# The norm of the third attention pair on VectorE, a new order of all work, and shifted operands of the 256-column products

## The chip, the cores and the metric

The kernel runs on one core of one Trainium2 chip. The time is device microseconds of one execution, and a kernel is compared by the median of its runs.

## The reference

Three stages follow each other: masked attention, a mixer of keys and receptance, and a block that mixes along the sequence and then along the channels. All inputs are float32 in value.

```python
scores = scale * np.matmul(q, k.transpose(0, 1, 3, 2))          # 4 x 8 heads, 576 x 64
scores = np.where(masks[None, :, :, :], scores, -1000000000.0)   # window 32, or 128 in steps of 4
attn = np.exp(scores - np.max(scores, axis=-1, keepdims=True))
attn = attn / (np.sum(attn, axis=-1, keepdims=True) + 1e-09)     # the norm
x = heads_side_by_side(np.matmul(attn, v))                       # 4 x 576 x 512
...
k = np.maximum(xk @ w_k, 0.0)                                    # xk, xr: x mixed with the row before
v = k * k @ w_v
y = (1.0 / (1.0 + np.exp(-(xr @ w_r)))) * v
...
u = y + (y.transpose(0, 2, 1) @ U @ V).transpose(0, 2, 1)
return u + np.maximum(u @ w_ch1, 0.0) @ w_ch2                    # 512 -> 2048 -> 512
```

## The kernel before

The work is recorded first and put in order afterwards. Every step of the program is an operation with its engine, its cost, and the keys that it reads and writes. `plan()` then issues all of them by one list schedule: each engine takes, among the next operations that are ready by a model of their times, the one with the lowest rank, and the ranks come from a long packed table, RANKED, with 3463 numbers. So RANKED sets what stands behind what on each of TensorE (PE), VectorE (DVE), ScalarE (ACT), GpSimd (POOL) and the DMA queue of SyncE (SP). Where the plan expects TensorE to wait over 350 ns, it puts products of a tile of zeros ahead of the next operation (L1707), 512 or 224 columns wide, for 0.8 of the expected wait; they write to a bank that is overwritten afterwards.

**Attention** works on units (a pair of heads of one batch element, cut into windows). The first four units go one by one: scores L854, transposes of the probabilities L907, the product with v L919. The later ones go two at a time: L955, L993, L1011. Between scores and transposes VectorE takes the row's minimum (L779), ScalarE the exponential with its sum (L788), VectorE the reciprocal (L793, L794), and one engine multiplies each window by it: `norm`, L797 to L805. On ScalarE that is one ACTIVATE for each of the eight windows (L800), on VectorE one TENSOR_TENSOR for each unit (L805). NORM_ENG[u // 2] names the engine, and its third entry covers units 4 and 5 alone, which are the first ones that go together.

**The mixer** runs over eight chunks of 288 columns. Its weights come as 64-bit floating point and are turned to 32 bits (L539 on VectorE, L540, L544 on ScalarE; wx is a whole weight of 512 columns). Chunk 0 is multiplied in plain float32 with whole weights (L1107, L1122, two passes of the array for each). For the other chunks weights and operands are split in a high and a low part, and a product is three passes: high weight by high operand, low by high, high by low (L1094, L1095, L1096). The sigmoid is L1156, one ACTIVATE over 1152 columns, and ScalarE loads a table ahead of it and another ahead of the next exponentials.

**The sequence mixing** takes y back from DRAM (ytmp, then yb by L1211 on SyncE's queue), transposes it (L1220), multiplies by U (L1238) and V (L1255), adds (L1263), and writes u to DRAM (uf). It is read back in blocks ub of two 256-column parts (L1295).

**The channel MLP** works on blocks of 256 columns (Q) with fewer products than the plain sum (a Strassen scheme). Its first layer is L1371 to L1373, its second L1459 to L1461, again high by high, low by high, high by low, each 128 x 128 weights by 256 columns. There are 3072 of these products, all after 339 us, and little else runs on TensorE from there on. The weights of column groups j with j % 4 < 3 lie in the mixer's weight pieces (wh, wl); those of the last group lie in two large tiles, box A and box B (names boxA, boxB). The moving operands lie in boxes raw, w64 (names boxraw, boxw), x, sig and B. `part(tag, i, unit, n)` cuts a box in units of 256 columns (1024 bytes), so that two operands of a product stand apart by a distance that, modulo 256 bytes, depends only on where the tiles begin. These beginnings follow from the sizes of the tiles allocated ahead of them; small pads (PADS) and a few unused columns set them.

## Time and profile before

| | us |
|---|---|
| three runs | 718.67, 718.71, 720.33 |
| median | 718.71 |
| the profiled execution | 722.05 |
| its span, first to last instruction | 720.3 |
| granted TensorE clock over the span, share of full speed | 0.998 |

The share of an engine's busy time is an average over stages that have different limits. So the windows and the waits of TensorE by stage are read beside the page, and the timeline where two starts are compared. The start of a TensorE product is recorded, its end is modelled; the pace of products is therefore taken from start to start.

### The profile page before, as it was taken

The numbers are of one execution on the slowest core, as the hardware profiler recorded it, in microseconds if no ns is written. First come the engines' busy times: TensorE is split into PE (matmuls) and PEld (weight loads), VectorE is DVE, ScalarE is ACT, GpSimd is POOL, SyncE is SP. The second block draws the span as 40 slices with busy tenths as digits, with TensorE's granted clock in tenths as the row PEclk, the third lists the DMA queues.
The fourth block names the chain that finished last, engine by engine and source line by source line (L and its number), as shares of the span: only waits on it lengthen the run. The fifth ranks groups of instructions, "written<-read, shape, count | busy, mean of one in ns | idle before, by whom it ended". The sixth has DMA issues, their size and how long they took to land.

```text
span 720.3 us, 19185 instructions
## 1 busy us (share of the span) xinstructions
PE 709.9 (99%) x7534; PEld 687.5 (95%) x7534; DVE 596.8 (83%) x1526; ACT 422.2 (59%) x1047; POOL 127.7 (18%) x164
## 2 busy tenths in 40 slices
PE   8999999999999999999999999999999999999997
PEld 6778999999999999999899999999999999999997
DVE  5888998788867645899998998999999899797953
ACT  5887886867685836275644543455486545454331
POOL 0101364646463724130000000000000000000000
PEclk9999999999999999999999999999999999999999
DMA  8976258776748430756546445552464114003222
GB/s 318 348 280 232 91 186 260 246 266 231 235 141 275 158 122 1 235 188 209 182 125 203 136 144 198 162 165 79 138 213 133 60 45 132 30 31 118 89 68 66
DMA packets 69979, 117.71 MB, mean 163 GB/s; under 512 B 6144, under 2 KB 41216, under 8 KB 69888
## 3 DMA queue, kind: packets, MB, share of 16 engines
q1 hardware_dynamic: 69888, 116.49, 48.8%
q8 instruction: 59, 0.97, 0.6%
q14 instruction: 32, 0.26, 0.1%
HBM read 85.00 MB, written 31.46 MB: 162 GB/s over the span
## 4 chain that ended last, share of the span: by engine, by line
PE 89%; DVE 5%; DMA 3%; issue 1%; ACT 1%; SPq 0%; DVEq 0%
PE psM L1094 10%; PE psM L1095 10%; PE psM L1096 10%; PE psM L1371 7%; PE psM L1372 7%; PE psM L1373 7%; PE psM L1122 4%; PE psS L1459 4%; PE psS L1460 4%; PE psS L1461 4%; PE psM L1460 4%; PE psM L1461 4%; PE psM L1459 3%; PE psS L1011 2%; PE psS L955 2%; PE psM L1107 1%
## 5 line engine op out<-in xcount | busy, mean ns | idle before, releaser
L1094 PE MATMUL psM<-xk,wh 128*128 128x288 f32 x336 | 100.3, 298 | 0.0
L1095 PE MATMUL psM<-xk,wl 128*128 128x288 f32 x336 | 99.1, 295 | 0.0
L1096 PE MATMUL psM<-xk,wh 128*128 128x288 f32 x336 | 99.0, 295 | 0.0
L1094 PE MATMUL psM<-k2s,wh 128*128 128x288 f32 x224 | 67.0, 299 | 0.0
L1095 PE MATMUL psM<-k2s,wl 128*128 128x288 f32 x224 | 66.1, 295 | 0.0
L1096 PE MATMUL psM<-k2s,wh 128*128 128x288 f32 x224 | 66.0, 295 | 0.0
L1094 PEld LDWEIGHTS psM<-xk,wh 128*128 128x128 f32 x336 | 63.2, 188 | 0.8
L1095 PEld LDWEIGHTS psM<-xk,wl 128*128 128x128 f32 x336 | 63.2, 188 | 0.2
L1096 PEld LDWEIGHTS psM<-xk,wh 128*128 128x128 f32 x336 | 63.2, 188 | 0.0
L1371 PE MATMUL psM<-boxraw,wh 128*128 128x256 f32 x198 | 55.9, 282 | 0.8 <-ACT hc L1441 0.5
L1373 PE MATMUL psM<-boxraw,wh 128*128 128x256 f32 x198 | 55.2, 279 | 0.0
L1372 PE MATMUL psM<-boxraw,wl 128*128 128x256 f32 x198 | 55.2, 279 | 0.0
L496 POOL TENSOR_TENSOR k2s<-k,k2s 128x288 fp32r<-128x288 f32 x49 | 42.9, 879 | 63.7 <-ACT k2s L501 24.0
L1461 PE MATMUL psS<-boxx,wh 128*128 128x256 f32 x192 | 53.7, 280 | 0.0
L1371 PE MATMUL psM<-boxw,wh 128*128 128x256 f32 x186 | 52.3, 281 | 0.2
L1373 PE MATMUL psM<-boxw,wh 128*128 128x256 f32 x186 | 52.0, 279 | 0.3 <-DVE boxw L498 0.3
L1372 PE MATMUL psM<-boxw,wl 128*128 128x256 f32 x186 | 51.8, 279 | 0.0
L788 ACT ACTIVATE pr<-pr,mn 128x64 f32<-128x64 f32 x144 | 48.0, 336 | 4.7 <-DVE mn L779 4.3
L496 POOL TENSOR_TENSOR xk<-m,xk 128x288 fp32r<-128x288 f32 x48 | 43.0, 905 | 36.2 <-ACT xk L501 26.1
L1094 PEld LDWEIGHTS psM<-k2s,wh 128*128 128x128 f32 x224 | 42.1, 188 | 0.6
L1170 DVE SCALAR_TENSOR_TENSOR k<-psM,rt 128x288 f32<-128x288 f32 x56 | 25.1, 454 | 20.9 <-ACT rt L1165 17.9
L1095 PEld LDWEIGHTS psM<-k2s,wl 128*128 128x128 f32 x224 | 42.1, 188 | 0.2
(255 smaller groups left out, 2486.6 us busy)
## 6 DMA issues: line engine op xcount, KB each, us to landing
w<-w2raw SPq DMA_DIRECT2D x32, 512.0 KB, 5.3
w<-w1raw SPq DMA_DIRECT2D x20, 512.0 KB, 7.3
w2f<-w SPq DMA_DIRECT2D x32, 256.0 KB, 3.5
ub<-uf SPq DMA_DIRECT2D x32, 256.0 KB, 3.3
ws<-w2f SPq DMA_DIRECT2D x24, 256.0 KB, 4.1
raw<-qk SPq DMA_DIRECT2D x16, 320.0 KB, 6.8
ytmp<-y SPq DMA_DIRECT2D x32, 144.0 KB, 2.1
yb<-ytmp SPq DMA_DIRECT2D x4, 1152.0 KB, 6.5
```

Of the source, the lines that this page charges most:

```text
L496: op("POOL", t, lambda: nc.gpsimd.tensor_tensor(out=out_(), in0=a(), in1=b(), op=ALU.subtract), r, w, 40, lock=True)
L788: nc.scalar.activation(pr[:, d : d + KW], pr[:, d : d + KW], AF.Exp, bias=mn[:, i : i + 1], scale=-1.0, accum_out=sm[:, i : i + 1])
L1094: nc.tensor.matmul(a, lhsT=wh, rhs=xh, start=start, stop=False)
L1095: nc.tensor.matmul(a, lhsT=wl, rhs=xh, start=False, stop=False)
L1096: nc.tensor.matmul(a, lhsT=wh, rhs=xl, start=False, stop=stop)
L1122: pe(2, MM1, lambda o=o, acc=accs[o]: nc.tensor.matmul(acc()[:, :HS], lhsT=whole_w[w]()[:, o * P : (o + 1) * P], rhs=cols(src, n), start=f ...
L1371: nc.tensor.matmul(a, lhsT=wh(*wi), rhs=xh(*ci), start=start and n == 1, stop=False, skip_group_check=True)
L1372: nc.tensor.matmul(a, lhsT=wl(*wi), rhs=xh(*ci), start=False, stop=False, skip_group_check=True)
L1373: nc.tensor.matmul(a, lhsT=wh(*wi), rhs=xl(*ci), start=False, stop=last, skip_group_check=True)
L1459: nc.tensor.matmul(a, lhsT=wh(*wi), rhs=xh(), start=start, stop=False, skip_group_check=True)
L1460: nc.tensor.matmul(a, lhsT=wl(*wi), rhs=xh(), start=False, stop=False, skip_group_check=True)
L1461: nc.tensor.matmul(a, lhsT=wh(*wi), rhs=xl(), start=False, stop=stop, skip_group_check=True)
```

## The change

The change has three parts: the norm of units 4 and 5 goes from ScalarE to VectorE; RANKED is a new table, and with it the whole order; and the sizes of a few tiles and the beginnings of the parts in box A (by 16 columns, 64 bytes) and box B (by 16 or 64 columns, 64 or 256 bytes) change.

```diff
-XCOLS = 584
+XCOLS = 592
-NORM_ENG = ("DVE", "DVE", "ACT", "DVE", "POOL")
+NORM_ENG = ("DVE", "DVE", "DVE", "DVE", "POOL")
 RANKED = (
-    'c-l3a2Y6M*635R?4+KK*AiadHgd#;iIwD1+i1gk&f*?&nsUq?~MXGe9NKvW;5J4dn=?GE<q)7>o<ldX}e*ZV;-S69P_w3Hj&d%=6PT6}o%yH5=j<blg-'
...
+    'c-l>y2Xs}%*2m9HZb%_?0|*Mz1w=r4?<&$1r6Wb8D@~Bzdy^(52m+5Hy?0Tnij+r{4$=t%p(G)s-Shqa?(^3A?pm|v%*>uWd-lxi*=26}bdD45IL<=SA'
...
-    mu_t = cp.tile([P, 24], F32, name="mu_t")[:, :8]
+    mu_t = cp.tile([P, 8], F32, name="mu_t")[:, :8]
...
-    PADS = ['w', 'pt']
+    PADS, PADW = ['w', 'pt'], {'w': 16, 'pt': 48}
...
-                    pool.tile([P, 16], F32, tag=f"pad{self.tag}", name=f"pad{self.tag}", bufs=1)
+                    pool.tile([P, PADW[self.tag]], F32, tag=f"pad{self.tag}", name=f"pad{self.tag}", bufs=1)
...
-        def __init__(self, home, c0, n):
-            self.home, self.c0, self.n = home, c0, n
+        def __init__(self, home, c0, n, shift=0):
+            self.home, self.c0, self.n, self.shift = home, c0, n, shift
...
-            return self.home()[:, self.c0 + a : self.c0 + (self.n if b is None else b)]
+            c0 = self.c0 + self.shift
+            return self.home()[:, c0 + a : c0 + (self.n if b is None else b)]
...
-    BOXES = {"A": (1, 4608), "B": (1, 4608), "raw": (4, 1280), "w64": (4, 1024), "x": (2, 2304), "sig": (1, 1152)}
+    BOXES = {"A": (1, 4624), "B": (1, 4672), "raw": (4, 1280), "w64": (4, 1024), "x": (2, 2304), "sig": (1, 1152)}
+    def SHIFT(tag, unit):
+        return 16 if tag == "A" else (16 if unit < 10 else 64) if tag == "B" else 0
...
-        return Part(boxes[tag, i], unit * Q, n * Q)
+        return Part(boxes[tag, i], unit * Q, n * Q, SHIFT(tag, unit))
...
-        return Part(x.home, x.c0 + a, b - a)
+        return Part(x.home, x.c0 + a, b - a, x.shift)
```

The distance of moving operand to weights, modulo 256 bytes, worked out from the addresses in the two programs as they are built, for the 3072 products of 256 columns:

| distance | before, first layer | before, second layer | after |
|---|---|---|---|
| 0 | 0 | 352 | 0 |
| 64 | 0 | 704 | 0 |
| 128 | 384 | 32 | 0 |
| 192 | 1152 | 448 | 3072 |

The first-layer products at 128 are those with weights in box A. For the 288-column products the distances are 64 and 192 in equal shares, in both.

The program's lines move by -1 up to L600, and by +3 from L620 on. The first place is TensorE at the start of the program, from the second product of zeros on (raw holds q, k and v of a unit, pr the probabilities, wx whole weights). Before:

```order
L1707 MATMUL psM<-zero 128x512 x2
L854 MATMUL psM<-raw 32x64 x20
L1707 MATMUL psM<-zero 128x512 x11
L854 MATMUL psM<-raw 32x64 x20
L907 MATMUL psS<-cst_t,pr 128x128 x3
L1707 MATMUL psS<-zero 128x512 x3
L919 MATMUL psS<-pts,raw 64x32 x20
L907 MATMUL psS<-cst_t,pr 128x128 x3
L854 MATMUL psM<-raw 32x64 x20
L1707 MATMUL psS<-zero 128x512 x3
L919 MATMUL psS<-pts,raw 64x32 x20
L907 MATMUL psS<-cst_t,pr 128x128 x3
```

After:

```order
L1710 MATMUL psM<-zero 128x512 x2
L857 MATMUL psM<-raw 32x64 x20
L1710 MATMUL psS<-zero 128x512 x9
L910 MATMUL psS<-cst_t,pr 128x128 x3
L857 MATMUL psM<-raw 32x64 x20
L922 MATMUL psS<-pts,raw 64x32 x20
L910 MATMUL psS<-cst_t,pr 128x128 x3
L857 MATMUL psM<-raw 32x64 x20
L1710 MATMUL psS<-zero 128x512 x2
L922 MATMUL psS<-pts,raw 64x32 x20
L1710 MATMUL psS<-zero 128x512 x3
L910 MATMUL psS<-cst_t,pr 128x128 x3
```

The transposes of unit 0 (L907, now L910) stand ahead of the scores of unit 2 (L854, now L857), and nine zero products stand ahead of them in place of eleven. The zero products in these rows are 19 before and 16 after; a few rows later three narrow ones (224 columns) are new.

The second place is ScalarE between 33 and 42 us of the trace, around the norm (rt and k are the first layer's results, pts the transposed probabilities, sg the sigmoid's tile). Before:

```order
L501 ACTIVATE sg<-psM 128x288 x4
L788 ACTIVATE pr,sm<-pr,mn 128x64 x8
L540 ACTIVATE wx<-wx 128x512
L800 ACTIVATE pr<-pr,sm 128x64 x8
L540 ACTIVATE wx<-wx 128x512
L1165 ACTIVATE rt<-psM 128x288
L540 ACTIVATE wx<-wx 128x512
L1165 ACTIVATE rt<-psM 128x288
L501 ACTIVATE pts<-psS 128x512
L1167 ACTIVATE k_693<-rt 128x288 x2
L1165 ACTIVATE rt<-psM 128x288
L1167 ACTIVATE k_693<-rt 128x288
```

After:

```order
L791 ACTIVATE pr,sm<-pr,mn 128x64 x4
L539 ACTIVATE wx<-wx 128x512
L791 ACTIVATE pr,sm<-pr,mn 128x64 x4
L539 ACTIVATE wx<-wx 128x512
L1168 ACTIVATE rt<-psM 128x288
L1170 ACTIVATE k_666<-rt 128x288
L1168 ACTIVATE rt<-psM 128x288
L1170 ACTIVATE k_666<-rt 128x288
L539 ACTIVATE wx<-wx 128x512
L500 ACTIVATE pts<-psS 128x512
L1159 ACT_TABLE_LOAD
L1159 ACTIVATE sg<-sg 128x1152
```

The eight L800 rows are gone (two TENSOR_TENSOR on VectorE take their place), and the sigmoid with its table load stands where before there were results of the mixer; before, it stands 20 rows further on, one row ahead of the conversion for which the second group of zero products is put in. A second table load, ahead of exponentials, stands nearer too. In the whole program ScalarE has 14 table loads after and 12 before.

The third place is TensorE where the sequence mixing of the last batch element meets the first products of the channel MLP. Before:

```order
L1373 MATMUL psM<-boxw_5527,wh 128x256
L1255 MATMUL psS<-vs,g 128x288 x4
L1707 MATMUL psS<-zero 128x512 x2
L1220 MATMUL psS<-cst_t,yb 128x128 x4
L1707 MATMUL psS<-zero 128x512 x6
L1238 MATMUL psS<-yh,us 128x512
L1238 MATMUL psS<-yl,us 128x512
L1220 MATMUL psS<-cst_t,yb 128x128 x8
L1371 MATMUL psM<-boxw_5337,wh 128x256
```

After:

```order
L1376 MATMUL psM<-boxw_5415,wh 128x256
L1258 MATMUL psS<-vs,g 128x288 x8
L1223 MATMUL psS<-cst_t,yb 128x128 x4
L1710 MATMUL psS<-zero 128x512 x5
L1241 MATMUL psS<-yh,us 128x512
L1241 MATMUL psS<-yl,us 128x512
L1223 MATMUL psS<-cst_t,yb 128x128 x4
L1374 MATMUL psM<-boxw_5370,wh 128x256
```

The eight products by V stand in one row rather than four and four, no zero products stand between them and the transposes of yb, and five rather than six stand behind these; of the twelve transposes that follow, four stand here and eight a few products later, where it was eight and then four. Ahead of this stretch, directly behind the last product of the mixer, eight transposes of the batch element before are added. On SyncE's queue two reads of ub stand ahead of the read of yb, where one stood.

## Rows read from the trace of the kernel before

**Rows 1.** page, busy time, share of the span and instructions of each engine.

```profile
PE 709.9 (99%) x7534; PEld 687.5 (95%) x7534; DVE 596.8 (83%) x1526; ACT 422.2 (59%) x1047; POOL 127.7 (18%) x164
```

**Rows 2.** page, the chain that ended last, by engine.

```profile
PE 89%; DVE 5%; DMA 3%; issue 1%; ACT 1%; SPq 0%; DVEq 0%
```

**Rows 3.** waits of PE: line, what it waited for, us in total, times, longest.

```profile
PE psM L1371 <- DVE hb L1421: 1.3, 1, 1.3
...
PE psS L1707 <- DVE us L1263: 0.9, 1, 0.9
```

**Rows 4.** windows: stretch, us, busy PE, PEld, DVE, ACT, POOL (instructions), granted clock, DMA, GB/s.

```profile
31.00:55.80 24.80, 24.80 (x362) 19.66 (x361) 19.60 (x81) 22.62 (x76) 1.43 (x3) 1.00 0.82 295
...
59.20:334.00 274.80, 274.80 (x3495) 267.82 (x3494) 213.65 (x640) 185.23 (x536) 121.24 (x150) 1.00 0.57 193
...
338.90:354.10 15.20, 13.25 (x84) 11.54 (x82) 14.03 (x33) 6.50 (x12) 0.00 (x0) 0.89 0.73 231
...
480.00:600.00 120.00, 120.00 (x1026) 119.95 (x1025) 113.02 (x230) 71.83 (x141) 0.00 (x0) 1.00 0.38 118
```

**Rows 5.** timeline of PE: start, us, line, output, moving and stationary operand, shape.

```profile
362.94 0.28 PE L1371 MATMUL psM<-boxw,boxA 128*128 128x256 f32 x1
...
364.26 0.28 PE L1373 MATMUL psM<-boxw,boxA 128*128 128x256 f32 x1
...
408.41 0.28 PE L1371 MATMUL psM<-boxw,wh 128*128 128x256 f32 x1
...
409.70 0.28 PE L1373 MATMUL psM<-boxraw,wh 128*128 128x256 f32 x1
...
538.01 0.28 PE L1371 MATMUL psM<-boxw,wh 128*128 128x256 f32 x1
...
539.26 0.28 PE L1373 MATMUL psM<-boxw,wh 128*128 128x256 f32 x1
...
705.00 0.28 PE L1459 MATMUL psS<-boxB,wh 128*128 128x256 f32 x1
...
713.48 0.28 PE L1459 MATMUL psM<-boxB 128*128 128x256 f32 x1
...
716.25 0.28 PE L1461 MATMUL psM<-boxB,boxA 128*128 128x256 f32 x1
```

**Rows 6.** timeline of PE, the start of the program: the zero products of L1707.

```profile
4.75 1.22 PE L1707 MATMUL psM<-zero 128*128 128x512 f32 x2
...
7.72 4.55 PE L1707 MATMUL psM<-zero 128*128 128x512 f32 x11
```

**Rows 7.** timeline of PE, the second group of zero products.

```profile
55.88 3.35 PE L1707 MATMUL psM<-zero 128*128 128x224 f32 x25
```

**Rows 8.** timeline of ScalarE just before that group.

```profile
52.46 1.28 ACT L1156 ACT_TABLE_LOAD   x1
...
53.75 1.16 ACT L1156 ACTIVATE sg<-sg 128x1152 f32<-128x1152 f32 x1
...
54.82 0.61 ACT L540 ACTIVATE wx<-wx 128x512 f32<-128x512 f32 x1
```

**Rows 9.** timeline of PE, from the last first-layer product to the channel MLP.

```profile
338.94 0.40 PE L1238 MATMUL psS<-yh,us 128*128 128x512 f32 x1
...
346.25 0.69 PE L1255 MATMUL psS<-vs,g 128*128 128x288 f32 x4
...
347.82 0.73 PE L1707 MATMUL psS<-zero 128*128 128x512 f32 x2 [0.88 <-DVE us L1263]
...
349.37 1.08 PE L1220 MATMUL psS<-cst_t,yb 128*128 128x128 f32 x4 [0.81 <-DMA yb<-ytmp]
...
350.10 2.90 PE L1707 MATMUL psS<-zero 128*128 128x512 f32 x6
```

**Rows 10.** timeline of ScalarE, the norm of units 4 and 5.

```profile
34.69 2.00 ACT L800 ACTIVATE pr<-pr,sm 128x64 f32<-128x64 f32 x8
```

**Rows 11.** timeline of VectorE, L805: instructions, shortest/median/longest ns, first and last start.

```profile
L805 DVE TENSOR_TENSOR pr<-pr,sm x2: 396/408/419, 45.5 to 45.8; 128x256 f32<-128x256 f32 x2
```

More of the change, by code (lines that the diff above doesn't have):

```diff
@@ new lines @@
+    'lG&4l1}j*ndZ84gB<5<s_RY-ah&b}*Zn5hb!WeH-2oXLry?*nf&G|N7`THeuG<rs9pH0)j`QM~>lUEAHPUf%0P_;~<4LaDkMxxC)GUtk3GKJzT=y%=*X'
+    'Xwvm{ue|>2K;f&|VX~QS@1r*>T<kZ>@OOJ;!*vp=%|8U-NwdTH{IK*&Jsy<5s5ckx<8(3GPpV9j6lgs)DmC6Rk(NI&-K9d~IMp<oj2~e#zV_0+$5b9@0'
+    'Q?Hz9Ya{|{*s{Zbh74zRB%cY&@-j6I6)3gDf|cWq$KB)V=S{OU!0N$?c~$3@MD@m>d}CTZ_0*DXcc-Sm$0QG)AUq2Fe{HP`8kv5UTS!BL<2H=yqq%;&W'
+    '*$GHw4&H&qm@>lfV2hIZ|(79Sa@s;Vg6Zj6Ly=(@@IUVb|3z%mO>iyyiV{E6rI^QM8-vI7U#;H#^*k^oy4H~C_cRXW70CNSJT2MEgy0@SU7C5uP(-Iy{'
+    'Bri-JLq8vI@sy`gzC&4ae@?!E{3T-~(7y<H8u8tl`aK|D3-M*3Z!P6%wD+Yy%jkSh-iz@^(msy?8&hr)u(?zP_8u@7$p1@f1-}XdGZOxsqx>n~=`}aU_'
@@ new lines @@
+    '}_}ULD04t+Uo&(6uc+ND+8AwhV5qFukkH@<aX>l^ro&Cc~(+-XzuBa*$5hQLdW;i{o>j$7i(UC_4yr~<+P8Pw9ZBd{O>}ax}>9wAI7*ffb9zGGUn3<Tr'
+    ';Sv53avRcPXdS*`aS!@?QeB-$v6Xg?SgI9M2r{(`OH``GLtzT?G721pipZxkh;p?dvFSA|-(L4s=~74}&Rt=>LP(k#vx{GQbz6-x1ORQW;V@Xv;`jUHa'
+    'Dtm&^A?#wtSkOtgaUFy9%$@tpDvzUx498TdP$wzc$I51v)zA47j-&TJ8wdW!Sd64^0?Js*l(2!&58$!9X*-i*_L?-s!S1Wm8Bmw@XH&fJXCntp@X3s0G'
+    'AbIM1OEiI;B8}cb^nu+vj2+T=nnnqq*`v}-;l*jW;=G+7KWb$gz`~;epP}aPneRkeAQ=Y|lGI$Ts_Y>A?C2)P<TZ0gjP0xV2#+-ECwI8wokJxeFqP_*+'
+    '%f0>l1F&zCIzmf5>PJ&IiE=yOeuS7I&?|&9$mdhn0Uj-8KmN`*I>)ckXD)3W$wBE<q^>yM9|OCabeXz1()-kxB>$aM8k)M%X9IPc!1IaZ5Mx|{&X)9jz'
@@ new lines @@
+    '&v7^Q-tJKu<eZ%AdjIw1^5e+b<h?I{^hg}23H-vGgG$(9NL=|sGmyzBYZcP+-Kc1_fw>IfeQxLAjasxyko$9l)OLdnpI<yPp40`)&_XVu<#J0`8IU!VX'
+    'v=-4`0H7e3Tc__730ksCxu$W2npR$>WyvDZqHy!F5dQMrz4-gCILQl4ozF+M4tQen-G$(j3ZrNsk%(Gs=HZUtDsP@_y18#ux*wWf{8&ZQ;NM$nTLCr>z'
+    '2gb^+Ipl$rYS%;_BPof-EGZ95tB19&qWI>%F2%x`B}b3O}vdio6j*CU^u>C)s8)P?FS>5c*ZCFM9z9+f5aqW|-N-L<nRPo}(_a!1k?zwz=0brtFVr?&@'
+    'YQNN5jj*ioWF}h2Jkq*)R8}KJ-Pa`h{oh!*Z(KZ+0JP`XXeP)sV>$AHf9drB=m?hxd&H9BRyMtMmi_m$6_T0ez>h&1_{uhz~z;A%wv5d2qJ_mulKwCp{'
+    'ofpZz%;b+H$En*1Y);WYzeAGie&h4c;QmHuhFtndd&ySPZTer(`cZ#dvX}38*6a#vF;ViEy|e|Hw~+aiV;{EDJpkON;A~F0A@zkaA@{)j9ecDn?UM67n'
@@ new lines @@
+    'cEBcj!v_4m4&(%;H!r`dH_ugC1+FYo=>m63?0P+CNsCvCzH+&FssS`q3sQLA^BMxJd!KD=u;Bd6~VSYF927E@{E9;(b~Xu2hT#<A2LRnS0=O0=ze4!-X'
+    'hIs9!<cLNWPkK1aO1-&dK-Z<beLWhTnld2AazPn*)5qs9VZd1GJx|+wol}*ksdF#_kE+WSw*PGY39SqrMLHUx8PAKLz{-=y^%s?C@k4@aY))Aow2ey_~'
+    'jP?4fn!C8%F4{y|SI^4*kk@!d7m?kt_F?2LU*GC+G;Iwy4-8RI+Ps*vk`eS>t1KKsZIQ<qotkvCw><KWo<o#S-(fTK3~IM(jtP}5x=(65N}FX;CJH&3#'
+    'iw)5g&km*5tp!EqbX_D3890u&uG@H*^<`@QSQ(#w-x=LT7yo-DieJAq$3&fA%`xC~l&Uj<MKU{p{z6+t8iGC^Is{{US(0fg?oiR>A&qLbR(JnbUfx7XM'
+    'C+xFN;o$@AA7Iy#X9p&Uaryw48T?J*+cPe(D$KPTx^y$}{{ikClz*cC{Y<7Kr_wJoeWrk;hwgImh5BZ|^#P^<c`fvmhR`}39IKf_EcFSTjgHJs^Jzo>('
@@ L200 @@
+    ';8S}9sMWbTm8pC@A#R^H{qracA<VzoV~>vLjU)fuXIcCO17omv+7;9VmyZ+c5#aR-{wHT-m%^YGF|4p-+VlMbq}SQO(avIs%PWr-Tkm+`=5+-qVnXQYp'
+    '#BKgMLhJWEEafESY}#@6$&<i#I;-?$Pjo`4&Ee_q#mVdd0CfTzWUM+_kp~(rJtM?fukY?Pb5kBlN!j>0JK@6A#w?'
 )
```

153 lines of the change are left out of this document (65 added, 88 removed).

## The prediction

> **What bounds the kernel now.** I read the page first. TensorE is busy for 709.9 of 720.3 us [rows 1], and the chain that ended last is TensorE for 89%, VectorE for 5%, DMA for 3% [rows 2]. So a gain must either shorten TensorE's own work or take away one of the few places where it stands. The windows tell these stages apart [rows 4]. In 59 to 334 us TensorE fills the stretch whole (274.80 of 274.80), and again in 480 to 600 us (120.00 of 120.00): there nothing but the pace of its products counts. In 338.9 to 354.1 us it is busy for 13.25 of 15.20 us at a granted clock of 0.89, so the time goes into waits, fillers and a fallen clock. The waits view names few others: the largest is 1.3 us for a hidden block hb on VectorE, then 0.9 us for us [rows 3]. In 31 to 55.8 us TensorE is never idle (24.80 of 24.80), while ScalarE is busy for 22.62 of them; that is where the norm stands which the change moves.
>
> **The pace of the 256-column products.** In 480 to 600 us, where TensorE never waits, 1026 products take 120.00 us, 117.0 ns each [rows 4]. Between single starts the pace isn't one number [rows 5]. Twelve first-layer products with weights in box A, at distance 128, run from 362.94 to 364.26: 1.32 us over 11 steps, 120.0 ns. Twelve at distance 192 run from 408.41 to 409.70, 117.3 ns, but twelve others at 192 from 538.01 to 539.26, 113.6 ns. Seventy-two at 64, second layer, run from 705.00 to 713.48, 117.8 ns; the 23 behind them, at 0, take until 716.25, 120.4 ns. I did the same for all 3071 starts of the trace (these rows are the firsts and lasts of five of the runs), and left out steps over 130 ns. First layer: 115.9 ns at 192 (1136 steps), 118.3 at 128 (380). Second layer: 116.8 at 192 (446), 117.8 at 64 (702), 118.7 at 0 (349). All together: 117.1 ns. Which box holds an operand doesn't separate them further; the distance does.
>
> The change puts all 3072 at 192. Like for like, layer by layer, that is 384 x 2.4 ns for those at 128, 352 x 1.9 for those at 0, 704 x 1.0 for those at 64: 0.9 + 0.7 + 0.7 = 2.3 us less. I take **-2.3 us**. The bounds: nothing (0), if the tiles happen to differ by something other than distance, and, on the far side, what the two paces inside 192 allow. Its steps lie either near 113.5 or near 117.7 ns, some 40% in the first, whole runs of twelve in one of them, with nothing in the addresses to decide which; at the borders of runs the pace changes over. All in the fast pace would be 3072 x (117.1 - 113.4) = 11.4 us less, all in the slow one 3072 x 0.6 = 1.8 us more. As 40% is also what the share of changes each way inside 192 would settle at by itself (a fast step is followed by a slow one in 17% of cases, a slow by a fast one in 11%, which gives 0.11 / 0.28), I see no push to either end.
>
> The rows say that distance counts, at equal columns. The Trainium skill speaks against this part of the change: its page "SBUF — State Buffer", section "SBUF: two separate sides", says that on the engines' side only the port pair that VectorE and GpSimd share makes anyone wait, and TensorE never does; "TensorE: Matmul & The Clock Gate", section "Back-to-back issue gap", gives the gap from the number of columns alone. By that this term would be 0 and the sum 2.3 us higher, as in the second rival; the five runs of these rows, all of 256 columns at full clock, do not agree with one gap.
>
> **The start.** Up to 31 us TensorE waits for loads and for the softmax of single units, and the planner's zero products stand in these waits. Of these 19 wide ones precede the mixer's first product, 16 in the new order, and three narrow ones are added. Eleven wide ones take 4.55 us [rows 6], 0.41 each; a narrow one 3.35 / 25 = 0.13 [rows 7]: -3 x 0.41 + 3 x 0.13 = -0.84 us. Fillers stand for waits, so part returns as a wait for what they stood for: raw data that have not landed, or the minimum and exponentials of a unit. The bounds are 0 and -1.2 (the wide ones alone, none of it coming back). I take **-0.7 us**, as the transposes of unit 0 come at once behind the nine, where two zero products and a set of scores lay between.
>
> **The norm and the chunk-0 stage.** The eight ACTIVATEs cost ScalarE 2.00 us [rows 10]. Two TENSOR_TENSORs of the same form on VectorE are 396 and 419 ns at 45.5 us [rows 11]: 0.82 us, in a stretch where VectorE has 24.80 - 19.60 us free [rows 4]. By itself this is worth nothing at 35 us, since TensorE is never idle from 31 to 55.8 us: the work of chunk 0 covers it. It counts where that cover ends, at 55.88, where 25 zero products take 3.35 us [rows 7] until a whole weight is converted at 54.82, behind a table load of 1.28 and a sigmoid of 1.16 us [rows 8]. In the new order the sigmoid is 20 rows further ahead, and 21 zero products stand at the stop, 4 x 0.13 = 0.5 us less. Against it, another table load and exponentials now stand ahead of the weight that is waited for. With the 2.00 us that ScalarE no longer spends, the stop can shrink further. Bounds: all of the 3.35 us gone, or, on the other side, 1.28 + 1.16 + 1.28 = 3.7 us more from what has been put ahead. I take **-1.0 us**, nearer to the fillers' own count than to the end. Two more table loads in the program, 2 x 1.28 us, cost nothing where ScalarE has slack: it is busy for 185 of 275 us in 59 to 334 us [rows 4].
>
> **The passage to the channel MLP.** From 338.94, TensorE has three products by U, 48 of the first layer, then four products by V from 346.25, and stands for the sums us (0.88 us and two zero products, 0.73); yb lands for the transposes at 349.37, 0.81 us after TensorE is ready, and six zero products take 2.90 us, 0.48 each at a fallen clock [rows 9]. Waits and fillers here are 0.88 + 0.73 + 0.81 + 2.90 = 5.3 us. In the new order the same work and eight transposes more come in a row: 48 x 0.116 + 0.7 (the products by U) + 2 x 0.69 + 8 x 0.09 (half of what one of the four from 349.37 to 350.10 takes at the fallen clock) = 8.4 us, to 347.3. If yb lands as it does now, 10.4 us behind 338.94, TensorE is idle for 2.0 us and then has five zero products, 2.4 us: 4.4 us, a gain of 0.9. The idle time is in one piece, unfilled, so the clock may fall earlier than now; I take **-0.6 us**. Bounds: -2 (yb released sooner) and +2 (yb behind two reads of ub on SyncE's queue, rather than one, and landing later). Later, the wait for hb and those for DVE's other blocks, some 3 us together up to 480 us, may move either way; the order alone doesn't tell, and I put them at 0 with 1.5 us to each side. VectorE is nearly full there (14.03 of 15.20, and 113.02 of 120.00 us [rows 4]), so a faster TensorE meets it sooner; in 480 to 600 us it has 7 us left, three times what the pace would take.
>
> The tail behind the last product is the same work, 0.
>
> **Sum.** -2.3 - 0.7 - 1.0 - 0.6 = -4.6 us. The profiled execution took 722.05 us and its span is 720.3; it lies 3.3 us above the median of the three runs, 718.71. Against its own time the sum is 717.4; against the median, to which the new median is compared, **714.1 us**.
>
> **Rivals.** First, the stream holds its fast pace. Products at other distances often throw it from one pace into the other now: all 31 + 13 fast steps that follow a change of distance from 192 to 0 or 128 are preceded by slow ones. Without such neighbours it might stay at 113.4: -11.4 - 2.3 = 705.0 us if throughout, about 709 if in two thirds of the steps. Against it: inside 192 alone it falls back as often as it rises.
>
> Second, the distance isn't what counts, and the first term is 0, or the stream holds the slow pace: 718.7 - 2.3 = 716.4 us, up to 718.2 with the slow pace. For it: two paces appear at one and the same distance, so that something else has a part. Against it: five means, from 350 to 1136 steps each, follow the distance in either layer.
>
> Third, the moves on ScalarE make it slower. Sigmoid, two table loads and four exponentials (some 5 us in all) stand ahead of the sixteenth weight, and the norm gives back only 2.00. If all of it comes behind the last zero product, TensorE stands for 5.0 us, unfilled, and its clock falls as it does in 338.9 to 354.1 us, where it costs some 1.7: with the other terms (-3.6) that is 718.7 - 3.6 + 5.0 + 1.7 = 721.8 us. It decides from a delay of about 4 us on. Against it: ScalarE has 2.2 us free in 31 to 55.8 us, and the sigmoid comes out of this very place.
>
> The change not doing what it says is no case here: the addresses and the order are those of the built program.
>
> **How the numbers follow.** Forecast 0.62, fast pace 0.13, pace term missing 0.18, slower through ScalarE 0.07. About 0.3%, 2.2 us, is what a measurement can tell from no change: below 716.5 is faster, above 720.9 slower. The forecast lies below 716.5 but for a few in a hundred, the second rival for a third: 0.59 + 0.13 + 0.06 = 0.78 faster, 0.15 within, 0.07 slower. The range leaves out the slower case, the upper half of the second rival and the fast pace beyond two thirds: 708.5 to 717.5 us.
>
> **What would show it.** Pace: 1026 products in 120.00 us become about 1034 per 120.00 in a stretch without waits, and start-to-start steps at one mean in both layers; if the mean stays at 117.0 the first term was wrong. Start: the mixer's first product comes 0.7 us earlier. Chunk 0: the second group of zero products ends with the product behind it starting at once. Passage: the time from the mixer's last product to the end of the zero products behind yb, now 350.10 + 2.90 - 338.94 = 14.1 us, is less by 0.6. It would be wrong above all if VectorE, nearly full up to 600 us, made new waits in the channel MLP.

## The result and the profile after

The changed kernel takes 714.28 us in the median of six runs (713.26 to 716.32), the one before 719.78 in the median of six (718.67 to 721.46). The ratio is 0.9918, with a 95% interval of 0.9899 to 0.9936: 5.9 us less, between 4.6 and 7.3. On another chip (e12_after, below) it was 0.9920 (0.9903 to 0.9937). Forecast was 714.1 us, 4.6 us less, range 708.5 to 717.5. The profiled executions lie further apart than the medians (spans 711.8 and 720.3 us); below, two things are shown in which single executions of one kernel differ, by some 2 us each.

The page of the changed kernel, its waits of TensorE (line, what it waited for, us in total, times, longest), and three windows of it (stretch, us, busy PE with instructions, granted clock, DMA share, GB/s); they answer to [rows 1], [rows 3] and [rows 4]:

```profile
PE 703.4 (99%) x7527; PEld 681.2 (96%) x7527; DVE 598.0 (84%) x1528; ACT 421.4 (59%) x1041; POOL 125.9 (18%) x164
```

```profile
PE psS L1258 <- DVE us L1266: 1.1, 1, 1.1
...
PE psS L1223 <- DMA yb<-ytmp: 0.6, 1, 0.6
PE psM L1374 <- DVE hb L1424: 0.5, 1, 0.5
```

```profile
410.00:520.00 110.00, 110.00 (x937) 1.00 0.50 160
668.00:707.00 39.00, 39.00 (x347) 1.00 0.22 67
...
480.00:600.00 120.00, 120.00 (x1025) 1.00 0.33 102
```

TensorE is still the bound. The first two windows hold nothing but 256-column products, all of them at distance 192, on a TensorE that never waits at full clock. In the first a product takes 110.00 / 937 = 117.4 ns, in the second 39.00 / 347 = 112.4 (from the starts in the timeline 117.8 and 113.3; a window counts products that it cuts). So one kernel, in one execution, at one distance, runs at two paces, and each for tens of microseconds: some 970 steps in a row in the first, 352 in the second. Before the change both appear too, but at 192 in runs of a dozen or two [rows 5].

The third window is the one that the prediction named as its sign for the pace: 1034 products were forecast there, 1026 stood there before [rows 4], and 1025 stand there now. By that sign alone the pace would not have changed. But two thirds of this window lie in two long runs at the slow pace (up to 521.7 us, and from 541.6 to 578.2); over all the steps counted below, the mean falls from 117.1 to 115.7 ns. In the second trace (e12_after) the same window has 1032.

Three places that the prediction had named, in the timeline of the changed kernel (start, us, engine, line, output, operands, count). The zero products at the start, the mixer's first product, and the three new narrow zero products, which stand behind it, against [rows 6]; then the mixer's first product before:

```profile
7.54 4.10 PE L1710 MATMUL psS<-zero 128*128 128x512 f32 x9
...
17.96 2.11 PE L1110 MATMUL psM<-xk,wx 128*128 128x288 f32 x8
...
21.59 0.57 PE L1710 MATMUL psM<-zero 128*128 128x224 f32 x3
```

```profile
19.02 2.11 PE L1107 MATMUL psM<-xk,wx 128*128 128x288 f32 x8
```

The second group of zero products and the product behind it, against [rows 7]; then the last step of the whole weight that this product reads, which is VectorE's, after and before, and the product before:

```profile
51.00 2.71 PE L1710 MATMUL psM<-zero 128*128 128x224 f32 x21
53.55 3.75 PE L1125 MATMUL psM<-k,wx 128*128 128x288 f32 x14
```

```profile
52.63 0.69 DVE L549 SCALAR_TENSOR_TENSOR wx<-w,wx 128x512 int32<-128x512 int32 x1
```

```profile
57.56 0.69 DVE L550 SCALAR_TENSOR_TENSOR wx<-w,wx 128x512 int32<-128x512 int32 x1
```

```profile
59.08 11.33 PE L1122 MATMUL psM<-k,wx 128*128 128x288 f32 x46
```

ScalarE ahead of it, against [rows 8]:

```profile
37.45 1.28 ACT L1159 ACT_TABLE_LOAD   x1
38.74 1.17 ACT L1159 ACTIVATE sg<-sg 128x1152 f32<-128x1152 f32 x1
...
48.67 1.28 ACT L791 ACT_TABLE_LOAD   x1
```

The passage to the channel MLP, against [rows 9]:

```profile
348.15 0.63 PE L1223 MATMUL psS<-cst_t,yb 128*128 128x128 f32 x4 [0.62 <-DMA yb<-ytmp]
348.54 1.41 PE L1710 MATMUL psS<-zero 128*128 128x512 f32 x5
```

The norm of units 4 and 5 is now two instructions of VectorE, ahead of where ScalarE did it [rows 10]:

```profile
33.50 0.42 DVE L808 TENSOR_TENSOR pr<-pr,sm 128x256 f32<-128x256 f32 x1
...
35.26 0.42 DVE L808 TENSOR_TENSOR pr<-pr,sm 128x256 f32<-128x256 f32 x1
```

### The profile page after: what moved, and what is told of

The parts are those of the page before. It is cut to its first block, busy times and chain, and to the rows that moved or that the text cites. A ratio compares the mean times of both kernels' runs of the same rounds, so it can differ in the third digit from the quotient of the medians.

```text
span 711.8 us, 19151 instructions
## 1 busy us (share of the span) xinstructions
PE 703.4 (99%) x7527; PEld 681.2 (96%) x7527; DVE 598.0 (84%) x1528; ACT 421.4 (59%) x1041; POOL 125.9 (18%) x164
## 5 line engine op out<-in xcount | busy, mean ns | idle before, releaser
L1376 PE MATMUL psM<-boxw,wh 128*128 128x256 f32 x186 | 51.9, 279 | 0.0
L1375 PE MATMUL psM<-boxw,wl 128*128 128x256 f32 x186 | 51.9, 279 | 0.0
L1097 PEld LDWEIGHTS psM<-k2s,wh 128*128 128x128 f32 x224 | 42.1, 188 | 0.4
L1099 PEld LDWEIGHTS psM<-k2s,wh 128*128 128x128 f32 x224 | 42.1, 188 | 0.0
```

The costliest lines, as they stand in the source:

```text
L1097: nc.tensor.matmul(a, lhsT=wh, rhs=xh, start=start, stop=False)
L1099: nc.tensor.matmul(a, lhsT=wh, rhs=xl, start=False, stop=stop)
L1375: nc.tensor.matmul(a, lhsT=wl(*wi), rhs=xh(*ci), start=False, stop=False, skip_group_check=True)
L1376: nc.tensor.matmul(a, lhsT=wh(*wi), rhs=xl(*ci), start=False, stop=last, skip_group_check=True)
```

## The experiments

### The parts apart: distance alone, order alone, distance 0

e1_addr is the kernel before with the beginnings of tiles changed and nothing else; every engine's order stays word for word. e2_order is the changed kernel with the tiles at their old places. e5_all0 is the changed kernel with all 256-column products at distance 0:

```diff
-    PADS, PADW = ['w', 'pt'], {'w': 16, 'pt': 48}
+    PADS, PADW = [], {}
-    BOXES = {"A": (1, 4624), "B": (1, 4672), ...
+    BOXES = {"A": (1, 4608), "B": (1, 4608), ...
-        return 16 if tag == "A" else (16 if unit < 10 else 64) if tag == "B" else 0
+        return 0
```

Expected of e1_addr: 

> The kernel before with the changed beginnings of tiles alone: every instruction stands where it stood on every engine, and all 3072 products of 256 columns are at distance 192. If the distance sets their pace, the mean step falls from 117.1 to the 115.7 ns that the changed kernel shows, 3072 x 1.4 = 4.4 us, and the median by 4 to 5 us; by my prediction's like-for-like term, 2.3 us. If the order decides whether the stream holds its fast pace, the second layer's mean stays near 116.8 ns and the gain near 2.3 us. If the distance is only a bystander, nothing changes.

Expected of e2_order: 

> The changed kernel with the tiles at their old places: new order and norm on VectorE, distances as before. If the distance is worth 4.4 us and the parts add, it is 1 to 2 us faster than before and some 4 us slower than the changed kernel; the start (1.0 us) and the passage to the channel MLP (1.4 us) come earlier as in the changed kernel's trace, and the mean step of the 256-column products is 117.1 ns. If the order makes the pace, the mean step is 115.7 ns and it is as fast as the changed kernel.

Expected of e5_all0: 

> The changed kernel, same instructions in the same order, with all 256-column products at distance 0 rather than 192 (the 288-column ones move too, from 64 and 192 to 0 and 128). If distance sets the pace, the mean step is 118.7 to 120 ns, so 3072 x 3 to 4.3 ns = 9 to 13 us more than the changed kernel, some 4 to 7 us over before. If uniformity is what helps (no neighbours at other distances), it is about as fast as the changed kernel. If neither, it equals the kernel with the old places, some 4 us over the changed one.

| kernel | median us | of before, with interval |
|---|---|---|
| e1_addr, old order, all at 192 | 720.3 (717.08 to 726.87, 12 runs) | 0.9992 (0.9968 to 1.0015) |
| e2_order, new order, old distances | 717.66 (717.25 to 719.75) | 0.9956 (0.9940 to 0.9973) |
| changed kernel | 714.28 | 0.9918 (0.9899 to 0.9936) |
| e5_all0, new order, all at 0 | 726.18 | 1.0070 (1.0047 to 1.0093) |

Distance 0 against 192, at the same order, is worth 1.0070 - 0.9918 = 1.5% of the time, some 11 us, as was expected of distance. About 1.6 us of it stands in the mixer (270.0 us against 268.4), where the 288-column products move too. The mean step of its 256-column products in the trace is 119.9 ns, and of 3042 steps only nine, never two in a row, are below 115.5. That no reading by uniformity alone can explain. The windows of its trace and of the one before (same columns), in stretches that TensorE fills whole, e5_all0 first:

```profile
480.00:600.00 120.00, 120.00 (x1000) 1.00 0.35 105
600.00:700.00 100.00, 100.00 (x835) 1.00 0.23 72
```

```profile
600.00:700.00 100.00, 100.00 (x855) 1.00 0.21 67
```

120.00 / 1000 is 120.0 ns, and 100.00 / 835 is 119.8, against 100.00 / 855 = 117.0 before.

The order alone gives 0.44%, 3.2 us. The distance on top of it gives 0.9956 - 0.9918 = 0.38%, 2.7 us. For e2_order I had expected 1 to 2 us from the order and some 4 us from the distance on top. The distance under the old order gives 0.08%, which can't be told from nothing (0.15% more to 0.32% less), nor from 0.38%, since both are differences of medians with intervals of some 0.2% to each side. My expectation of 2.3 to 5 us for e1_addr missed, though its trace shows about the pace expected: a mean step of 115.3 ns, against 117.1 before. But that traced execution took 717.08 us, the least of the twelve.

### Where the pace gained goes

e1b_addr is the same kernel as e1_addr, for a second trace. 

> The same kernel as e1_addr, for a second trace, because its twelve times spread from 717.1 to 726.9 us. If the stream's pace differs from execution to execution (the phase that it settles in), the mean step of the 256-column products differs from the 115.3 ns of the first trace, toward 117. If the spread is in waits, the mean step is again 115.3 ns and the difference stands in a few waits between 338 and 480 us, where VectorE is nearly full.

The first reading holds: its mean step is 116.1 ns, not 115.3, so the pace does differ from execution to execution. The waits don't make this difference: e1b_addr, the slower of the two, has the smaller ones. But both have more than the kernel before. From the 49th 256-column product to the last, worked out from the starts of the timelines: n = 3023 steps times the mean of those under 130 ns; what the longer ones take above that mean; the rest is the few other products.

| trace | mean step, ns | all steps at it, us | above it, us (steps) | whole stretch, us |
|---|---|---|---|---|
| before | 117.1 | 354.1 | 4.7 (24) | 362.2 |
| e9_dve_there (below) | 117.2 | 354.2 | 3.4 (22) | 361.1 |
| e1_addr | 115.3 | 348.6 | 6.8 (52) | 358.9 |
| e1b_addr | 116.1 | 350.8 | 5.2 (42) | 359.5 |
| e2_order | 117.0 | 353.7 | 2.4 (21) | 360.1 |
| changed kernel | 115.7 | 349.6 | 3.0 (29) | 356.8 |
| changed kernel, second trace | 115.7 | 349.7 | 5.2 (44) | 359.1 |
| e8_act_there (below) | 114.9 | 347.5 | 5.1 (43) | 356.7 |
| e11_kick (below) | 115.3 | 348.5 | 3.6 (35) | 356.3 |
| e5_all0 | 119.9 | 362.5 | 1.6 (15) | 368.0 |

(The second trace is that of e12_after, below.) At 192 the stalls are larger than at the old distances, and at 0 they are smallest. By what the trace names as ended last, VectorE and ScalarE end nearly all of them (4.4 of the 4.7 us before, 4.9 of the 5.2 in the second trace): TensorE meets the blocks that these two make for it sooner, and part of the time comes back as waits. Under the old order the distance takes 354.2 to 349.7 us in the mean of two traces each, 4.5 us less, and the stalls grow by 2.0. Under the new one it takes 353.7 to 348.9 (mean of three, against the one trace of e2_order), 4.8 less, and the stalls grow by 2.0 too. The size of what comes back is rough: two traces of the changed kernel, both at 115.7 ns, have 3.0 and 5.2 us of stalls. The waits of TensorE in e1_addr, beside those of before [rows 3]:

```profile
PE psS L1711 <- DVE us L1267: 0.9, 1, 0.9
PE psS L1224 <- DMA yb<-ytmp: 0.9, 1, 0.9
PE psM L1375 <- DVE hb L1425: 0.9, 2, 0.6
PE psM L1375 <- ACT hc L501: 0.5, 1, 0.5
PE psM L1375 <- ACT hc L1445: 0.5, 1, 0.5
PE psM L1377 <- DVE boxw L498: 0.3, 1, 0.3
```

The two traced executions of e1_addr would make it 2.5 us faster than before in this stretch, its median over twelve makes it 0.9. Some of its untraced runs took 722 to 727 us at granted clocks from 0.992 to 0.999 over the span, so the clock fell in some of them for a while; where and behind which wait, no trace shows, and why the median of e1_addr shows so little of the gain stays open.

### The norm alone

e3_norm changes NORM_ENG under the old table. e9_dve_there makes the kernel before issue the two VectorE instructions at the very place of the eight ACTIVATEs, with the plan unaware of it, so that no other row moves; e8_act_there does the reverse in the changed kernel.

```diff
 e3_norm
-NORM_ENG = ("DVE", "DVE", "ACT", "DVE", "POOL")
+NORM_ENG = ("DVE", "DVE", "DVE", "DVE", "POOL")
 e9_dve_there
-            op("ACT", 60 + n * 245, lambda: fn(eng), r, w, 140)
+            op("ACT", 60 + n * 245, lambda: fn("DVE"), r, w, 140)
 e8_act_there
-            op("DVE", 125 * k - 50 + 1.04 * n * KW, lambda: fn(eng), r, w, 80, lock=True)
+            op("DVE", 125 * k - 50 + 1.04 * n * KW, lambda: fn("ACT" if u // 2 == 2 else eng), r, w, 80, lock=True)
```

Expected of e3_norm: 

> The kernel before with the norm of units 4 and 5 on VectorE, under the old table of ranks (the schedule shifts a few rows, 24 on TensorE). My theory: hidden, within 0.5 us of before, since TensorE has no wait from 31 to 55.8 us, and the 2 us that ScalarE gains go into its wait. The rival: ScalarE is the bound of chunk 0 and the zero products at 55.9 us end 1 to 2 us sooner, with as much off the time.

Expected of e9_dve_there: 

> The kernel before with the norm of units 4 and 5 issued on VectorE at the very place of the order where ScalarE did it: nothing else moves on any engine, so unlike in e3_norm the plan doesn't lay out new zero products. My theory: the step is hidden, within 0.7 us of before in the median, the zero products at 55.9 us end where they did, since their end is set by the weight's arrival and their own number. The rival: ScalarE bounds chunk 0, and TensorE passes 70 us 1 to 2 us earlier.

Expected of e8_act_there: 

> The changed kernel with the norm of units 4 and 5 back on ScalarE at the very place where VectorE does it now: no other move. My theory: within 0.7 us of the changed kernel (some 5.5 us under before), so the norm is what the new order was laid out for, and no source of time by itself. The rival: the new order has ScalarE so full at 33 to 50 us that 2.00 us more there delay the weights: 1 to 2 us slower than the changed kernel, seen as a wait of TensorE near 51 to 55 us.

e9_dve_there: 719.5 us, 1.0006 of before (0.9992 to 1.0020): under the old order the step was hidden. Its 25 zero products take as long as ever [rows 7], 1.4 us later, by which its start was later:

```profile
57.33 3.29 PE L1707 MATMUL psM<-zero 128*128 128x224 f32 x25
```

e8_act_there: 714.95 us, 0.9940 (0.9918 to 0.9962), on another chip than the changed kernel's 0.9918 (0.9899 to 0.9936). That is some 1.5 us more than the changed kernel, where I had expected at most 0.7, but the two intervals overlap, so the times alone don't settle it. The trace speaks for the rival: TensorE waits for a result that ScalarE empties from its bank only behind the first half of the norm, and the transposes of the probabilities start 0.7 us later than in the changed kernel. First e8_act_there, then the changed kernel:

```profile
36.24 0.75 PE L1125 MATMUL psM<-xk,wx 128*128 128x288 f32 x2 [0.39 <-ACT rt L1168]
36.83 1.17 PE L996 MATMUL psS<-cst_t,pr 128*128 128x128 f32 x4
```

```profile
36.11 0.60 PE L996 MATMUL psS<-cst_t,pr 128*128 128x128 f32 x4
```

The last two of the four transposes wait for ScalarE's second half of the norm, which ends at 37.62, so that the four take until 37.83 rather than 36.55, and everything behind them stays some 1.3 us later up to the first split product. The rival had put this at 51 to 55 us; it stands at 36. It is one trace.

e3_norm: 729.6 us, 1.0121 (1.0095 to 1.0146), 8.7 us slower. I had expected at most 0.5 us. The plan, run with another duration on another engine under ranks that were made for the old one, puts things elsewhere, expects waits and fills them:

```profile
71.39 5.96 PE L1707 MATMUL psM<-zero 128*128 128x512 f32 x25 [0.41 <-DVE y L1188]
...
201.46 2.11 PE L1707 MATMUL psM<-zero 128*128 128x512 f32 x8
...
203.99 1.66 PE L1707 MATMUL psM<-zero 128*128 128x512 f32 x6 [0.43 <-issue]
```

84 zero products stand in it (68 on psM, 16 on psS), 52 before. So the norm on VectorE was no source of time under the old order, and with the old table it cost 9 us. Under the new order, which has put other work of ScalarE in its place, the one trace of e8_act_there prices it at some 1.3 us; the rest of what the new order gave has to be read in the order.

### The pace by itself

e6_paces is a kernel of products alone, on constant operands: 96 of 256 columns at each of eight distances, then 48 of 288, then 96 of 256 in another sequence of distances. 

> Only products, on constant operands, nothing of the reference is computed: 96 products of 256 columns at each of eight distances (0, 32, ... 224 bytes mod 256), in the pattern of the channel MLP (three products for each pair of split operands, weights loaded for each), in two orders, and 48 of 288 columns at each. If distance alone sets the pace, each segment has one pace, the same in both orders: 192 below 64 (by 2 ns or more) and 64 below 0 and 128 (117.7 against 118.5 to 120). If the two paces are a phase that survives from segment to segment, a segment at 192 is either near 113.5 or 117.7 by what ran before it, so the two orders differ. The 288-column segments show one pace of 132 ns at all distances.

Its timeline (start, us, operands with xa, xc, xe, xg, xb, xd, xf, xh for 0, 64, 128, 192, 32, 96, 160, 224 bytes; 96 products each):

```profile
26.09 11.47 PE L37 MATMUL bk<-xc,wgt 128*128 128x256 f32 x96
37.40 11.55 PE L37 MATMUL bk<-xe,wgt 128*128 128x256 f32 x96
48.78 11.05 PE L37 MATMUL bk<-xg,wgt 128*128 128x256 f32 x96
59.68 11.37 PE L37 MATMUL bk<-xb,wgt 128*128 128x256 f32 x96
70.88 11.68 PE L37 MATMUL bk<-xd,wgt 128*128 128x256 f32 x96
82.40 11.55 PE L37 MATMUL bk<-xf,wgt 128*128 128x256 f32 x96
93.78 11.53 PE L37 MATMUL bk<-xh,wgt 128*128 128x256 f32 x96
```

From start to start over 96 (worked out in whole ns): 117.8 ns at 64, 118.6 at 128, 113.5 at 192, 116.7 at 32, 120.0 at 96, 118.6 at 160; and 120.0 at 0, 118.4 at 224 from their own starts. The second sequence gives each within 0.1 ns. No other engine works beside these products, and 192 is the best of the eight. In this kernel the weights always begin at 128 modulo 256 bytes, so by itself it can't tell the distance from the place of the moving operand. The programs as they are built settle that: at distance 192 the moving operand begins at 224, 160 and 64 modulo 256 in the kernel before, the changed kernel and e6_paces, and all three have steps of 113 to 114 ns, while the moving operands of e5_all0 begin at 160 too, at distance 0, and take 119.9. So it is the distance. With 288 columns the paces lie between 131.6 and 133.3 ns. But 192 showed only its fast pace here.

e7_phase asks what the slow one is: runs of 36 products at 192, each behind one product of another width; then 24 at 192 behind 12 at another distance. 

> Products only, nothing of the reference is computed. First 19 runs of 36 products of 256 columns at distance 192, each behind one product of another width (32 to 320 columns in steps of 16), then 24 products at 192 behind 12 at distance 0, 64, 128 and 32, six times each. If the pace is a phase that a disturbance sets, some of the runs hold 117.7 ns and the others 113.5, by the width ahead of them, and the neighbours at other distances leave the stream in either. If it returns by itself, all runs come back to 113.5 within a few products, and the slow runs of the kernel have a cause outside TensorE's operand stream.

Of 19 runs, one behind each width from 32 to 320 columns, 8 end fast and 11 slow, and each holds its pace from the seventh step on. Windows of two such runs (stretch, us, busy PE and PEld with products, VectorE, GpSimd, clock, DMA, GB/s), behind 128 and behind 208 columns:

```profile
45.60:49.70 4.10, 4.10 (x36) 4.10 (x36) 0.00 (x0) 0.00 (x0) 1.00 0.01 4
67.10:71.02 3.92, 3.92 (x36) 3.92 (x36) 0.00 (x0) 0.00 (x0) 1.00 0.00 0
```

4.10 against 3.92 us for 36: their steps go 117, 118, 118 and 113, 113, 114. So the pace is a phase in which the stream settles, set by what stood just ahead of it. All 24 runs behind twelve products at 0, 64, 128 or 32 came out fast within some six products; but all of them save the first also had a fast run ahead of the twelve.

e10_fine tries finer distances and shorter disturbances. 

> Products only, nothing of the reference is computed. At each of thirteen distances (16, 48, 80, 112, 144, 160, 176, 184, 192, 200, 208, 224, 240 bytes) 36 products behind one of 32 columns and 24 behind one of 208, which leave 192 in its slow and in its fast phase. My theory: 192 alone has two phases, near 113.5 and 117.7 ns; if a neighbour such as 176 or 208 runs at 113.5 behind both, it is the better distance. Then 12 products at 192, put in the slow phase, and behind them one, two or three at 64, 128, 0 or 32 with 12 more at 192: if a few products at another distance return the stream to its fast phase, the next 12 run at 113.5; if the whole run of twelve is needed, as in e7_phase, they stay at 117.7.

My hope for 176 or 208 failed: 119.1 to 119.5 ns at both. 200 and 184 are at 120 and over, so that 8 bytes beside 192 its pace is lost. Only 112 also gave 113.3 ns, and there a run that began at 117 to 123 came back to 113 by itself. (To put the kernel's products at 112 needs operands that begin at 16 bytes mod 32, and the tiles begin at multiples of 32. That was not tried.) Nor is one product ahead enough to tell the phase: behind one of 32 columns 192 was slow in e7_phase and in the runs that follow, and fast here. Behind a run in its slow phase, one product at another distance and twelve more at 192, three times over, 39 products in each window; the first with 64, then 128, then 32:

```profile
111.81:116.39 4.58, 4.58 (x41) 4.58 (x40) 0.00 (x0) 0.00 (x0) 1.00 0.00 0
131.23:135.70 4.47, 4.47 (x41) 4.47 (x40) 0.00 (x0) 0.00 (x0) 1.00 0.00 0
169.63:174.08 4.45, 4.45 (x41) 4.45 (x40) 0.00 (x0) 0.00 (x0) 1.00 0.00 0
```

64 leaves the stream at 117.8 ns, in all nine trials with one, two or three products; at 128 or 32, one to three products take it to 113.3 in six of six. At 0 it goes both ways: from the slow phase to the fast one in three of seven trials, and once, behind two products, from the fast phase to the slow one.

### Resets in the kernel

e11_kick uses that: 64 of the 3072 products at 32, the others at 192, all instructions where they were. e12_after is the changed kernel beside it.

```diff
-... "x": (2, 2304), ...
+... "x": (2, 2368), ...
-        return 16 if tag == "A" else (16 if unit < 10 else 64) if tag == "B" else 0
+        return 16 if tag == "A" else (16 if unit < 10 else 64) if tag == "B" else (64 if unit > 4 else 24 * (unit == 4)) if tag == "x" else 0
```

Expected of e11_kick: 

> The changed kernel, every instruction in its place, with 64 of the 3072 products of 256 columns at distance 32 and the other 3008 at 192: one low part in box x is moved by 96 bytes (the parts behind it by 256). In e10_fine one product at 32 took the stream from its slow phase to its fast one in every case. Theory: the 64 products act as resets, some 48 products apart, and the share of fast steps at 192 rises from 0.49 to 0.6 to 0.75; mean step 114.7 to 115.2 ns rather than 115.6, 1.5 to 3 us off TensorE's work, of which VectorE's waits give up to half back. The rival: the waits set the phase anew so often that the resets change nothing, or cost 0.5 us by their own pace.

Expected of e12_after: 

> The changed kernel again, beside the one with resets on the same chip, for a comparison of the two and a second trace. The median is 5 to 6 us under before; the mean step of its 256-column products lies between 115 and 116 ns, not at the value of the first trace, if the phase differs from execution to execution.

The fast share at 192 is 0.59 in its trace, against 0.48 in that of e12_after on the same chip, and the mean step 115.3 against 115.7 ns. That looks like the theory, but it isn't the resets. The 64 products stand in 36 groups of one to four; for the 29 groups with no stall around them, the six steps ahead can be compared with six steps behind. Seven groups met a slow stream, and one of them left it fast; 22 met a fast one, and 21 left it fast. And shares of 0.39 (e1b_addr) to 0.65 (e8_act_there) occur with no product at another distance. So what one product at 32 did in e10_fine it doesn't do in this kernel; why, no run shows. The time is the same, 714.11 us, 0.9922 of before (0.9908 to 0.9935), against 714.14, 0.9920 (0.9903 to 0.9937). The mean step of e12_after, 115.7 ns, is that of the first trace of the changed kernel, where I had expected another; the two differ in their stalls. That the pace differs between executions of one kernel rests on e1_addr and e1b_addr. No version tried here beats the changed kernel.

## Why the prediction was right, and where it was not

The time (714.1 forecast, 714.28 measured) was nearly met, the sum of its terms only partly. The near hit is partly luck: the median of the kernel before, with three runs more, is 719.78 us, not the 718.71 from which the forecast was counted, so that 4.6 us less was forecast and 5.9 measured. The stages of ten traces stand beside each other here, in us: the mixer's first product (start), from it to the first split product (chunk 0), the rest of the mixer, and from its last product to the 49th of the channel MLP (passage). The mean over four traces of the old order (before, e1_addr, e1b_addr, e9_dve_there) and six of the new one (changed kernel twice, e2_order, e8_act_there, e11_kick, and e5_all0, which is left out of the mixer, where it moves other products too):

| stage | old order | new order | difference | forecast |
|---|---|---|---|---|
| start | 19.4 (18.7 to 20.5) | 17.9 (17.5 to 18.4) | -1.5 | -0.7 |
| chunk 0 | 51.2 | 51.1 | -0.1 | -1.0 |
| mixer | 268.9 | 268.4 | -0.5 | 0 |
| passage | 13.9 (13.2 to 15.3) | 13.9 (13.4 to 15.0) | 0.0 | -0.6 |

**Pace, -2.3.** Right in mechanism and sign, and mis-sized: in traces it is 4.5 to 4.8 us, of which 2.0 come back. The step that failed is the like-for-like sum for the second layer. I took its 116.8 ns at 192 for what the others would reach. In the changed kernel it reaches 115.5 and 115.7 in two traces, with 52% and 48% of its steps fast rather than 22%, while the first layer stays where it was (115.9 before, 115.8 and 115.7). Before, its products at 192 stood among others at 0 and 64, most of them singly or in threes, and the steps around a change of distance are longer as the stream finds its phase: in e7_phase the first three steps at 192 behind a run at 0 take 121, 122 and 116 ns. A mean taken inside a mixture was not the pace of the pure stream. Next time the price would come from the longest pure runs, or from a kernel of products alone.

**What comes back.** I named it as the thing that would make the forecast wrong ("VectorE, nearly full up to 600 us"), and put it at nothing because VectorE had 7 us left in 120. A sum of free time over a stretch doesn't tell whether each block is ready when TensorE comes for it. Part of the gain comes back in every trace at 192, in the mean 2.0 of 4.6 us, and not in one place: 21 to 24 stalls become 29 to 52, each of up to 0.8 us. So the two errors, too small a pace and no return, cancelled, which is luck: 2.3 forecast, about 2.7 measured between e2_order and the changed kernel.

**The two paces.** "I see no push to either end" holds: over the traces with all products at 192 the share of fast steps is 0.39, 0.48, 0.49, 0.57 and 0.65, and 0.40 was taken. My first rival, a stream that holds its fast pace throughout, did not come about in the kernel, though e6_paces shows it in a kernel of products alone. e8_act_there comes near its two thirds in one execution, which took 715.12 us and not the 709 of that rival. The reason I gave for it, that neighbours at other distances throw the stream out of its fast pace, is neither borne out nor refuted: in e10_fine products at 32 and 128 bring it in, while of the two that stood in the second layer 64 leaves it slow and 0 does either. My second rival, that the distance isn't what counts, is out by e5_all0 and e6_paces.

**Start, -0.7.** Right in place, twice the size, and beyond the bound of -1.2. The wide zero products ahead of the mixer's first product take 7.5 us in the mean of the old order and 6.3 of the new, the full -1.2, and TensorE's idle time there falls from 1.3 to 0.9 us rather than growing: none of what was dropped came back as a wait. One trace makes much of the difference, e9_dve_there with 20.5; without it, it is -1.1. The 0.4 us for the three narrow products didn't belong here: they stand behind the mixer's first product.

**Chunk 0, -1.0.** Wrong. The stop at 55.88 moved to 51.00 and shrank from 3.35 to 2.71 us, but the end of the stage followed the start and nothing else. Two steps failed. The first is the count: four zero products fewer at the stop, but three more at 21.59, in the same stage, so 24 in place of 25. In this stage TensorE stands idle for 0.04 us or less in eight of the ten traces, so its length is that of TensorE's own work, 50.9 to 51.1 us in them; the two longer ones, e1b_addr (51.9) and e8_act_there (52.2), are the ones with idle time, 0.9 and 0.5 us. The second is the reading of the stop as a wait for ScalarE [rows 8]. The conversion at 54.82 ends at 55.44, before the first zero product; the weight's last step is VectorE's, and it is done at 58.26, 0.8 us before the product at 59.08. After, it is done at 53.32, 0.2 us before the product at 53.55. The zero products are fixed in number and run whether the weight has come or not, so a sooner weight can't shorten the stop, as e9_dve_there shows with 2.00 us off ScalarE. Whether fewer of them would was not tried. The rival by which ScalarE's moves make the kernel slower didn't come about; two table loads more cost nothing that can be seen.

**Passage, -0.6.** Wrong, for a reason in the reading. The clock of 0.89 and the 15.2 us of [rows 4] were an event of that one execution: other traces of the old order need 13.2 to 13.9 us at full clock, and one trace of the new order (e2_order, 15.0 us) shows the fallen clock in its turn. I priced a place from a single execution in which it was at its worst.

**Not forecast.** The order takes another 0.5 us off the mixer, and in the channel MLP the stalls above 130 ns fall from 4.1 us (mean of before and e9_dve_there) to 2.4 (e2_order), -1.7 us, less than the 2.2 by which two traces of the changed kernel differ. The order's own sum is then -1.5 - 0.1 - 0.5 - 1.7 = -3.8 us, beside 3.2 measured for e2_order and 2.3 forecast for these terms. I had put the waits for hb and its like at 0 with 1.5 us to each side, as the order alone doesn't tell.

By the Trainium skill's "SBUF — State Buffer", section "SBUF: two separate sides", only the port pair that VectorE and GpSimd share makes anyone wait on the engines' side, and TensorE never does. The runs don't go along with the conclusion that it then doesn't matter where TensorE's operands lie: e6_paces, with no other engine beside it, goes from 113.5 to 120.0 ns by the distance of its own two operands. And the gap that the Trainium skill's "TensorE: Matmul & The Clock Gate", section "Back-to-back issue gap", gives by the number of columns has one value for 256 columns, where these runs show 113.5 to 120.0 ns. By what mechanism the distance acts, no run shows.

## What to carry to other kernels

Where a stream of products of 256 columns, each with its own weights, bounds a kernel, find out how far apart its two operands lie modulo 256 bytes before anything else: between 192 and 0 it was worth 5% of the pace of the products (113.5 against 120.0 ns) and 1.5% of this kernel; against the old distances, with over half of the products at 192 already, 0.4% or less. It costs a few unused columns, and can be measured in a kernel of products alone. A fixed number of filler products sets the end of the stop that it fills once what it stands for is ready: find out when that is, down to its last step, before crediting a faster engine. A stage's gain on the bounding engine is paid out only as far as the engines that feed it have room: here some 2.0 of 4.6 us came back as waits. And one trace is one execution: price a stall or a fallen clock from several. Don't judge a move by itself under an order that was made for another: the norm was hidden under the old order and stands on TensorE's path in the one trace under the new.

## What the runs showed of the hardware

- A product of 256 columns in float32r with its own weight load takes 113.3 to 121.7 ns at full clock, by the distance of its moving operand to its weights modulo 256 bytes: fast at 192 and at 112, 120 and more at 0, 96, 184 and 200 (e6_paces, e10_fine).
- At 192 the stream has two steady phases, 113.3 and 117.8 ns a step. It stays in one for up to some 970 products, and what stands ahead of it, such as one product of another width, can set either (e7_phase). In e10_fine one to three products at 32 or 128 took it from the slow to the fast one in six of six cases, at 64 in none of nine, at 0 in three of seven; in the kernel with products at 32 among those at 192 (e11_kick), one of seven groups did.
- One phase or the other thus decides some 4.5 us per thousand products. Two executions of one kernel, e1_addr and e1b_addr, differ by 2.2 us in it.
